# Half of the k and v loads moved to GpSimd's queue, in half batches, with a new order of work, in a linear-attention kernel with a gated convolution

## The chip, the cores and the metric

The kernel runs on one core of a Trainium2 chip. The metric is the device time of one execution in microseconds (us), here the median of three runs. A profile belongs to one execution; its "span" is the stretch between the first and the last instruction that the profiler saw.

The engines are called PE (matmul; PEld is its weight load), DVE (VectorE), ACT (ScalarE), POOL (GpSimd) and SP (SyncE, which issues transfers only). L12 is line 12 of the kernel's file.

## The reference

Two layers follow each other. Four batches, 8 heads, 768 steps, 48 channels a head:

```
for t in range(768):
    y[t]  = r[t] . (state + (u * k[t]) (x) v[t])      # per batch and head
    state = w * state + k[t] (x) v[t]                 # state is 48 x 48
x        = y, heads side by side: (4, 768, 384)
gate_pre = sum over 5 taps of conv_w[k] * x[t - 4 + k]    # causal
out      = (sigmoid(gate_pre) * (x @ w_val)) @ w_out      # both weights 384 x 384
```

Inputs and output are float32.

## The kernel before, in words

**Units.** A batch has three units of 256 steps, so there are twelve, n = 0 to 11; batch 0 is units 0 to 2, batch 1 is 3 to 5, batch 2 is 6 to 8 and batch 3 is 9 to 11. For units 2 to 11 a unit is two chunks of 128 steps; units 0 and 1 (n < TWO) place even and odd steps in neighbouring columns instead, which gives longer contiguous pieces in memory.

**What one unit needs**, by the names in the order string:

- `r:n`, `k:n`, `v:n`: loads of its rows into `r_st`, `k_st`, `v_st`. `k:4.1` is the second chunk of unit 4. A unit of r comes in pieces of 384 bytes (two steps); a chunk of k or v in 1,024 pieces of 192 bytes (one step of one head), L322.
- `RS`, `KS`: r and k times powers of the decay, to bf16 (L328, L342). `RT`, `KT`: transposes on PE (L353, L366); `RE`, `KE`: their copies out of PSUM (L297, L299).
- `PR`, `S`, `SE`: the bonus r.u.k (L402, L416). `DV`: v times this bonus (L430, L438). `CV`: v to bf16.
- `A`: attention scores within a chunk (L479), `M`: their mask (L489). `KV`, `ZI`, `ZE`: the running state (L516, L526, L536). `YD`, `YI`, `YZ`, `YE`: the unit's output from bonus, chunk and state (L561, L572), copied into `xT`.

**The second layer** works on seven pieces of up to 512 steps: `C` convolution (L664), `G` sigmoid (L675), `V` value product (L682), `HT` their product (L692), `O` output product (L705), `OE` its copy, `st` the store (L721); `OH`, `OF`, `sf` are the same in halves at the end (L732). `wv` and `wo` load the two weights, `WV` and `WO` cast them (`wval`, `wout`). `D:0.12` is filler on PE, twelve units of 128 columns (L737). `ER`, `EJ`, `EK` compute the tables of decay powers on ACT, from `w`. `CG` builds diagonal matrices for the convolution.

**What sets the order.** Every engine works in program order, and the whole program is one string, ORDER, found by a search and written out; each token is one stage. The ending names the engine: `/V` VectorE, `/P` GpSimd, `/A` ScalarE, `/S` SyncE; a number behind @ is the PSUM bank. An instruction that waits holds up everything behind it on its engine. A transfer's issue too is an instruction of its engine, so a load on SyncE's queue stands behind all earlier loads and stores there.

**Buffers.** `k_st` and `v_st` are rings of six tiles, a tile for one unit (NLD = 6, L61 to L65); `r_st` likewise. A load into a ring waits until the unit six before it has been read.

All loads and stores before are issued by SyncE, but for two stores at the end on ScalarE's queue.

Of the kernel before, what the change touches and what calls it, by code (L numbers as in the profile page):

```python
# [8 lines left out]
F32 = mybir.dt.float32  # L9
# [6 lines left out]
def kernel(  # L16
# [14 lines left out]
    B, H, S, D = r.shape  # L31
# [14 lines left out]

    TWO = 2
# [9 lines left out]
    def ring(name, shape, n, dtype=BF16):  # L57
# [245 lines left out]
    def pairs(t_):  # L303
        return t_.rearrange("p c h d -> p (c h d)").rearrange("p (h s d) -> p h s d", s=2, d=D)
# [33 lines left out]
    def scale_k(eng, n, c):  # L338
        if n < TWO:
            return scale_rows(eng, ks_t[n % NKS], pairs(k_st[n % NLD]), dj, c)  # L340
        cs = cut(c, 2)
        eng.tensor_tensor(  # L342
            out=ks_t[n % NKS][:, cs, :, :, 0:D].rearrange("p c n a d -> p c (n a) d"),
            in0=k_st[n % NLD][:, cs],
            in1=dk[:, cs],
            op=ALU.mult,
        )
# [80 lines left out]
    def bonus_v(eng, n):  # L428
        if n < TWO:
            return eng.tensor_tensor(  # L430
                out=dv_t[n % NDV].rearrange("p s (h d) -> p h s d", d=D),
                in0=pairs(v_st[n % NLD]),
                in1=s_t[n % NDV].rearrange("p s h -> p h s")[:, :, :, None].to_broadcast(
                    [128, H, 2, D]
                ),
                op=ALU.mult,
            )
        eng.tensor_tensor(  # L438
            out=dv_t[n % NDV].rearrange("p c (h d) -> p (c h) d", d=D),
            in0=v_st[n % NLD].rearrange("p c h d -> p (c h) d"),  # L440
            in1=s_t[n % NDV].rearrange("p s h -> p (s h)")[:, :, None].to_broadcast(
                [128, 2 * H, D]
            ),
# [290 lines left out]
    def dummy(m, b):  # L734
# [13 lines left out]
        w/S TE CD CP ML ZR/P ZV/V MK r:0.1/S k:0.0/S D:0.12@0 LN:.1 WS:.1@1 wp/S r:1/S r:0.0/S LN:.0 WS:.0@0  # L748
        SC ER:.2@1 k:0.1/S cw/S k:1/S u/S D:1.24@2 ER:.0@0 ZM/V ZK/V EJ:.3@1 ID r:2/S ER:.3@1 EK:.3@1
        RS:0.1/V k:2.0/S v:0/S k:2.1/S ER:.1@0 EJ:.2@1 EK:.2@1 v:1/S r:3/S k:3.0/S k:3.1/S EJ:.1@0 EJ:.0@0  # L750
        wv/S D:2.1@1 RS:1/V RT:0.1@3 EK:.1@0 v:2.1/S v:2.0/S k:4.1/S D:3.1@1 D:4.12@2 wo/S RS:0.0/V RT:0.0@1
        ZX/V RE:0.1@3/A r:4/S v:3.1/S k:4.0/S v:3.0/S RE:0.0@1/A KS:0.1/V KT:0.1@2 KE:0.1@2/A EK:.0@0 CB
        KS:0.0/V IT KT:0.0@3 KS:1/V k:5.0/S r:5/S v:4.0/S v:4.1/S WT@1 WC@1 RS:2/P KE:0.0@3/V CT@4 WM RT:1@5
        A:0.1@06 k:5.1/S CE@4 r:6/S PR:0.1@2 PR:0.0@3 k:6.0/S v:5.1/S k:6.1/S v:5.0/S UW@1 r:7/S k:7.1/S
        A:0.0@47 KT:1@2 RE:1@5/A S:0@1 CG:.0/P M:0.1@7 M:0.3@6 M:0.0@4 SE:0@1/A DV:0/P k:7.0/S RT:2@5 CV:0/A
        v:6.1/S v:6.0/S RE:2@5/A PR:1@2 D:5.2@1 D:6.12@7 M:0.2@0 KS:2/V KE:1@2/A S:1@7 CG:.2/P D:7.2@4
        YD:0@04 KV:0@51 ZE:0.0@5/V SE:1@7/V A:1.1@26 TS CV:1/A YI:0@04 M:1.2@2 KT:2@7 A:1.0@25 M:1.3@6
        YE:0.0@0/A ZI:0.1@1 RS:3/P YZ:0.1@4 KV:1@06 PR:2@7 DV:1/P KE:2@7/A S:2@3 ZE:0.1@1/V v:7.1/S k:8.1/S
        k:8.0/S r:8/S v:7.0/S ZI:1.0@0 M:1.1@5 RT:3@1 M:1.0@2 A:2.1@75 SE:2@3/A ZE:1.0@0/V M:2.3@5 CG:.1/P
# [24 lines left out]
        st:3.2/S ZE:7.1@6/V O:3.3@4 st:2.0/S O:3.1@0 M:8.1@1 CV:8/P KV:8.0@2 KS:9/P ZI:8.0@2 KT:9@6 KE:9@6/A
        OE:3.3@4/A st:3.3/S DV:8/P YD:8.0@1 M:8.2@5 ZE:8.0@2/V YD:8.1@3 OE:3.1@0/V YI:7.1@7 YI:8.0@1 PR:9@6
        YI:8.1@3 YZ:8.0@1 YZ:8.1@3 YZ:7.1@7 A:9.0@40 YE:8.0@1/A A:9.1@62 S:9@1 YE:8.1@3/A YE:7.1@7/V M:9.3@2
        M:9.2@6 O:3.0@3 RS:10/P RT:10@7 M:9.1@0 M:9.0@4 KS:10/P SE:9@1/V DV:9/P V:4.0@2 CV:9/A OE:3.0@3/A
        V:4.1@6 KT:10@0 RE:10@7/A KV:9.0@1 C:4@453 G:4.1@5 ZE:9.0@1/V KE:10@0/V PR:10@0 KV:9.1@1 V:4.2@7
        ZE:9.1@1/V S:10@5 YD:9.0@0 YD:9.1@1 YI:9.1@1 G:4.0@4 HT:4.1@6 st:3.0/S SE:10@5/A YI:9.0@0 YZ:9.1@1
        HT:4.0@2 G:4.2@3 YE:9.0@0/A HT:4.2@7 A:10.0@36 RS:11/P A:10.1@25 RT:11@0 M:10.0@3 CV:10/A O:4.3@7  # L790
        KV:10.0@3 ZI:10.0@3 M:10.2@2 RE:11@0/A ZE:10.0@3/V OE:4.3@7/A YE:9.1@1/A KS:11.0/P KT:11.0@4
        PR:11.0@4 DV:10/P KE:11.0@4/A O:4.1@2 OE:4.1@2/A O:4.2@0 M:10.1@6 KV:10.1@3 M:10.3@5 YD:10.1@1
        KS:11.1/P KT:11.1@7 YD:10.0@6 YZ:10.0@6 YI:10.0@6 YZ:10.1@1 YI:10.1@1 PR:11.1@7 KE:11.1@7/V S:11@5
        ZE:10.1@3/V YE:10.0@6/A YE:10.1@1/A A:11.0@67 M:11.1@7 SE:11@5/A DV:11/P st:2.3/S st:2.1/S st:4.3/S
        A:11.1@24 C:5@513 CV:11.0/A KV:11.0@7 OE:4.2@0/A V:5.2@0 M:11.0@6 ZI:11.0@7 G:5.1@1 V:5.1@1 G:5.2@3
        G:5.0@5 YD:11.0@3 V:5.0@5 M:11.3@4 YD:11.1@4 st:3.1/S YZ:11.0@3 M:11.2@2 HT:5.2@0 ZE:11.0@7/V
# [117 lines left out]
```

## Time and profile before

| | |
|---|---|
| median of three runs | 96.81 us (96.21 to 103.59) |
| the profiled execution | 96.63 us |
| its span | 94.9 us |
| read from HBM, written to it | 15.35 MB, 4.72 MB |
| loads of k in chunks, 192 KB each | 22 on SyncE's queue |
| loads of v in chunks, 192 KB each | 20 on SyncE's queue |
| stores, 192 KB each | 22 on SyncE's queue |
| busy on GpSimd: `rs` x10, `dv` x10 and x2, `ks` x7 and x2 | 18.2, 14.7 and 3.0, 12.7 and 2.0 us |

How to read the profile's lines. In the page's first part each engine has its busy time, its share of the span and its instructions. The second part cuts the span into 40 slices of 2.4 us; each digit is a busy share in tenths. A line of a group or a timeline names the line of code, the engine, the operation, the output and input tiles, shapes (partitions x elements) and a count; in brackets stands the idle time of the engine just before, and what ended it. "A <- B: 4.1, 3, 1.7" says that A waited for B for 4.1 us in total, three times, 1.7 us at most. An issue line ends with the median time from issue to landing. SPq is an issue on SyncE's queue.

### The profile page before, as it was taken

What the parts mean: (1) busy time and instruction counts of PE and PEld (TensorE: products, weight loads), DVE (VectorE), ACT (ScalarE), POOL (GpSimd) and SP (SyncE); (2) the same over time, 40 slices, a digit from 0 to 9 for tenths busy, and PEclk for the clock granted to TensorE, in tenths of its full rate; (3) what the DMA queues carried; (4) which work ended last, traced back from release to release, by engine and by line L of the source; (5) the groups of instructions that cost most, each with busy time, mean ns of one, the idle gap of its engine ahead of it and who ended that gap; (6) DMA issues with size and microseconds to landing.
All of it is one profiled execution on the core that took longest, in us unless ns stands there. A gap on an engine that the chain in (4) does not pass through costs nothing.

```text
span 94.9 us, 4608 instructions
## 1 busy us (share of the span) xinstructions
PE 84.0 (89%) x1973; PEld 58.9 (62%) x1979; DVE 78.6 (83%) x163; ACT 60.5 (64%) x119; POOL 59.7 (63%) x61
## 2 busy tenths in 40 slices
PE   5998977986795789799999899999999999999950
PEld 1545746755584456578757687587867778666630
DVE  5889999899455299989899969899997999989430
ACT  6597879784935646654797544835991897632740
POOL 6600499795809467698899899997918990800000
PEclk9999999999999999999999999999999999999999
DMA  0799999993759699898989999969997898950473
GB/s 4 191 297 310 284 267 226 214 276 67 199 149 270 128 261 211 200 219 170 258 175 215 231 259 211 228 179 271 224 240 161 286 228 316 364 200 11 166 286 129
DMA packets 62936, 20.36 MB, mean 214 GB/s; under 512 B 58814, under 2 KB 62916, under 8 KB 62916
## 3 DMA queue, kind: packets, MB, share of 16 engines
q1 hardware_dynamic: 62628, 19.88, 85.0%
q8 instruction: 15, 0.25, 1.1%
q10 hardware_dynamic: 288, 0.20, 0.6%
q14 instruction: 5, 0.04, 0.1%
HBM read 15.35 MB, written 4.72 MB: 211 GB/s over the span
## 4 chain that ended last, share of the span: by engine, by line
PE 37%; SPq 27%; DVE 12%; DMA 11%; POOL 4%; issue 4%; ACT 1%; ACTq 0%; POOLq 0%; DVEq 0%
SPq L322 16%; DMA k_st<-in_k_dram 11%; PE PS L705 7%; PE PS L572 6%; PE PS L682 6%; SPq L309 5%; PE PS L664 5%; POOL dv L438 3%; PE PS L479 3%; SPq L277 3%; DVE hT L692 3%; PE PS L561 2%; PE PS L353 2%; PE PS L516 2%; PE PS L366 2%
## 5 line engine op out<-in xcount | busy, mean ns | idle before, releaser
L489 DVE TENSOR_TENSOR at<-PS,mask 128x512 bf16<-128x512 f32 x48 | 30.4, 683 | 1.9 <-PE PS L479 1.4
L328 POOL TENSOR_TENSOR rs<-r_st,dr 128x768 bf16<-128x768 f32 x10 | 18.2, 1816 | 9.8 <-PE PS L353 6.8
L438 POOL TENSOR_TENSOR dv<-v_st,s_sb 128x768 bf16<-128x768 f32 x10 | 14.7, 1475 | 9.1 <-DMA v_st<-in_v_dram 4.1
L692 DVE TENSOR_TENSOR hT<-PS,gate 128x512 bf16<-128x512 f32 (+1 forms) x21 | 12.1, 610 | 4.4 <-PE PS L682 2.6
L705 PE MATMUL PS<-wout,hT 128*128 128x384 bf16 (+1 forms) x78 | 14.2, 314 | 1.5 <-POOL wout L299 1.0
L342 POOL TENSOR_TENSOR ks<-k_st,dk 128x768 bf16<-128x768 f32 (+1 forms) x9 | 14.7, 1635 | 0.9 <-DMA k_st<-in_k_dram 0.9
L297 ACT CAST xT<-PS 128x384 bf16<-128x384 f32 x20 | 9.0, 482 | 9.6 <-PE PS L572 9.4
L675 ACT ACTIVATE gate<-PS 128x512 bf16<-128x512 f32 (+1 forms) x21 | 10.3, 538 | 7.3 <-PE PS L664 6.6
L682 PE MATMUL PS<-xT,wval 128*128 128x512 bf16 (+1 forms) x57 | 13.8, 345 | 0.3
L297 ACT COPY rT<-PS 128x1024 bf16<-128x1024 bf16 (+1 forms) x13 | 12.3, 948 | 2.4 <-PE PS L353 2.4
L297 ACT COPY o<-PS 128x384 f32<-128x384 f32 (+1 forms) x19 | 8.5, 469 | 3.6 <-PE PS L705 3.5
L705 PEld LDWEIGHTS <-hT 128*128 128x128 bf16 x78 | 6.9, 97 | 5.4 <-issue 2.2
L297 ACT CAST vb<-v_st 128x768 bf16<-128x768 f32 (+1 forms) x10 | 8.0, 804 | 2.8 <-DMA v_st<-in_v_dram 2.6
L353 PE MATMUL PS<-ident,rs 128*128 128x128 bf16 x96 | 7.8, 224 | 0.9 <-POOL rs L328 0.9
L572 PE MATMUL PS<-at,vb 128*32 128x128 bf16 (+1 forms) x448 | 8.5, 220 | 0.0
L664 PE MATMUL PS<-xT,cwd 32*32 32x512 bf16 (+1 forms) x420 | 8.1, 346 | 0.0
L737 PE MATMUL PS<-some 128*128 128x512 bf16 (+2 forms) x19 | 6.8, 499 | 1.1 <-DVE some L142 1.1
L366 PE MATMUL PS<-ident,ks 128*128 128x128 bf16 x80 | 6.3, 219 | 1.4 <-ACT gate L675 0.9
L353 PEld LDWEIGHTS <-rs 128*128 128x128 bf16 x96 | 6.0, 100 | 2.5 <-POOL rs L328 1.1
L297 ACT COPY kT<-PS 128x1024 bf16<-128x1024 bf16 (+1 forms) x7 | 6.2, 890 | 1.9 <-PE PS L366 1.2
L682 PEld LDWEIGHTS <-wval 128*128 128x128 bf16 x63 | 5.4, 97 | 3.1 <-POOL wval L299 0.2
L536 DVE TENSOR_TENSOR z<-PS,bdm 128x384 bf16<-128x384 f32 x12 | 6.6, 553 | 1.0 <-PE PS L516 0.6
(89 smaller groups left out, 141.1 us busy)
## 6 DMA issues: line engine op xcount, KB each, us to landing
k_st<-in_k_dram SPq DMA_DIRECT2D x22, 192.0 KB, 4.3
r_st<-in_r_dram SPq DMA_DIRECT2D x11, 384.0 KB, 4.2
out_dram<-o SPq DMA_DIRECT2D x22, 192.0 KB, 3.8
v_st<-in_v_dram SPq DMA_DIRECT2D x20, 192.0 KB, 4.6
v_st<-in_v_dram SPq DMA_DIRECT2D x2, 384.0 KB, 5.1
wv_st<-in_moe_w_val_dram SPq DMA_DIRECT2D x1, 576.0 KB, 6.7
r_st<-in_r_dram SPq DMA_DIRECT2D x2, 192.0 KB, 3.5
k_st<-in_k_dram SPq DMA_DIRECT2D x1, 384.0 KB
```

Of the source, the lines that this page charges most:

```text
L297: eng.copy(out=dst, in_=src)
L322: q.dma_start(out=dst[n % len(dst)][:, c], in_=x[b, :, t0 : t0 + C, :].rearrange("h p d -> p h d"))
L328: eng.tensor_tensor(out=dst[:, :, ns, :, 0:D].rearrange("p s n a d -> p (n a) s d"), in0=src[:, hs], in1=tab[:, hs], op=ALU.mult,)
L342: eng.tensor_tensor(out=ks_t[n % NKS][:, cs, :, :, 0:D].rearrange("p c n a d -> p c (n a) d"), in0=k_st[n % NLD][:, cs], in1=dk[:, cs], op ...
L353: nc.tensor.transpose(bank16(b)[:, c0 : c0 + 128], src[:, s, i].rearrange("p a x -> p (a x)"), ident)
L438: eng.tensor_tensor(out=dv_t[n % NDV].rearrange("p c (h d) -> p (c h) d", d=D), in0=v_st[n % NLD].rearrange("p c h d -> p (c h) d"), in1=s ...
L489: nc.vector.tensor_tensor(out=at_t[n % NAT][:, c, a], in0=bank(b).rearrange("p (n x) -> p n x", x=128), in1=(mask2[:, c, None, :] if n < T ...
L572: nc.tensor.matmul(out=PS[32 * q : 32 * q + 32, b, 128 * T : 128 * T + 128], lhsT=lt, rhs=rh, start=False, stop=last, skip_group_check=True,)
L664: nc.tensor.matmul(out=halves(PS[32 * qo : 32 * qo + 32, b[T], 0:N], m), lhsT=cwd[rows, T, t, :], rhs=columns(xT[rows, T], m, PAD - t), st ...
L682: nc.tensor.matmul(out=halves(bank(b, N), m), lhsT=wval[:, kt, T, :], rhs=columns(xT[:, kt], m, 0), start=(kt == 0), stop=(kt == NT - 1),)
L692: nc.vector.tensor_tensor(out=hT_t[m % NHT][:, T, 0:N], in0=bank(b, N), in1=gate_t[m % NG][:, T, 0:N], op=ALU.mult,)
L705: nc.tensor.matmul(out=bank(b)[:, c], lhsT=hT_t[m % NHT][:, T, i * C : i * C + C], rhs=wout[:, T, c], start=(T == 0), stop=(T == NT - 1),)
```

## The change

The rings of k and v change from six tiles of a unit to two tiles of a batch (NLD = 2), with the head as the outer index within a partition. For units below BY = 6 a load writes its columns of the batch's tile, with the same pieces as before. For batches 2 and 3 a load brings four heads of a whole batch: `k:6.0`, `k:6.1`, `k:9.0`, `k:9.1` and the same of v, eight loads of 576 KB, each of 24 pieces of 192 bytes in each of the 128 partitions. They are issued by GpSimd, and so are six more loads: r:1, r:2, v:0, v:1, k:2.0 and k:3.1. The stages that read k and v take their columns from the batch's tile. The order string is a new one throughout; work has been handed between engines in it, too (`WO` and all of `WV` to ScalarE, `RS:3`, `RS:4`, `RS:10`, `DV:5`, `DV:8` to VectorE, the zeros of `rs` to VectorE and those of `xT` to GpSimd).

```
+    BY = 6
     TWO = 2
...
     NLD, NRL, NKS, NRS, NVB, NDV, NRT, NKT, NPR, NAT, NZ, NG, NHT, NO = (
-        6, 6, 3, 2, 4, 2, 3, 2, 2, 3, 6, 2, 2, 12
+        2, 6, 3, 2, 4, 2, 3, 2, 2, 3, 6, 2, 2, 12
     )
     r_st = ring("r_st", [128, H, 2, D], NRL, F32)
-    k_st = ring("k_st", [128, 2, H, D], NLD, F32)
-    v_st = ring("v_st", [128, 2, H, D], NLD, F32)
+    k_st = ring("k_st", [128, H, 2 * NU, D], NLD, F32)
+    v_st = ring("v_st", [128, H, 2 * NU, D], NLD, F32)
...
-    def pairs(t_):
-        return t_.rearrange("p c h d -> p (c h d)").rearrange("p (h s d) -> p h s d", s=2, d=D)
+    def unit(ts, n):
+        b, cu = divmod(n, NU)
+        return ts[b % len(ts)][:, :, 2 * cu : 2 * cu + 2, :]
+
+    def by_chunk(ts, n):
+        return unit(ts, n).rearrange("p h c d -> p c h d")
...
     def load_kv(dst, x, n, c, q):
         if n < TWO:
-            return load_rows(pairs(dst[n % len(dst)]), x, n, q, c)
+            return load_rows(unit(dst, n), x, n, q, c)
         b, cu = divmod(n, NU)
-        t0 = cu * W + c * C
+        if n < BY:
+            t0 = cu * W + c * C
+            return q.dma_start(
+                out=unit(dst, n)[:, :, c, :], in_=x[b, :, t0 : t0 + C, :].rearrange("h p d -> p h d")
+            )
+        hs = cut(c, H)
         q.dma_start(
-            out=dst[n % len(dst)][:, c], in_=x[b, :, t0 : t0 + C, :].rearrange("h p d -> p h d")
+            out=dst[b % NLD][:, hs].rearrange("p h c d -> p (h c) d"),
+            in_=x[b, hs].rearrange("h (c p) d -> p (h c) d", p=C),
         )
```

`scale_k`, `bonus_v` and `cast_v` read `unit(...)` or `by_chunk(...)` where they read `pairs(...)` or the tile itself.

GpSimd's queue in the new order, in program order (a colon marks a unit; loads in bold):

constants and masks, **r:1, v:0, r:2, k:3.1, v:1, k:2.0**, CV:0, RS:2, CG:.0, CG:.1, WM, DV:0, KS:2, CG:.2, **k:6.0**, KS:3, DV:1, DV:2, **v:6.1, v:6.0, k:6.1**, KS:5, DV:3, RS:5, DV:4, RS:6, KS:6, RS:7, CV:7, KS:7, **k:9.1, k:9.0**, KS:8, RS:8, DV:6, RS:9, DV:7, KS:9, **v:9.1, v:9.0**, KS:11.1, RS:11, KS:10, CV:11.1, KS:11.0, DV:9, DV:10, DV:11.

SyncE's queue begins with w, k:0.0, k:0.1, cw, k:1, wp, r:0.0, u, r:0.1, k:3.0, v:2.0, wv, k:4.0, k:2.1, wo, r:3, v:2.1, v:3.0, v:4.1, v:3.1, k:5.1, v:4.0, r:4, k:4.1, k:5.0, v:5.0, r:5, v:5.1, r:6; from there it holds r:7 to r:11 and the stores.

In the order before, the first real tokens and the last k and v loads were:

```
w/S TE CD CP ML ZR/P ZV/V MK r:0.1/S k:0.0/S D:0.12@0 LN:.1 WS:.1@1 wp/S r:1/S r:0.0/S LN:.0 WS:.0@0
...
M:6.0@4 O:2.2@4 ZI:5.0@1 M:6.2@3 RE:7@7/A O:2.1@3 KV:6.0@2 KS:7/P M:6.3@5 DV:5/P v:11.0/S M:6.1@6
OE:2.2@4/A OE:2.1@3/A v:11.1/S YD:5.0@5 YD:5.1@7 ZE:5.0@1/V KT:7@6 ZE:6.0@2/V PR:7@6 DV:6/P YD:6.0@1
```

More of the change, by code (lines that the diff above doesn't have):

```diff
@@ L339, in scale_k @@
         if n < TWO:
-            return scale_rows(eng, ks_t[n % NKS], pairs(k_st[n % NLD]), dj, c)
+            return scale_rows(eng, ks_t[n % NKS], unit(k_st, n), dj, c)
         cs = cut(c, 2)
@@ L343, in scale_k @@
             out=ks_t[n % NKS][:, cs, :, :, 0:D].rearrange("p c n a d -> p c (n a) d"),
-            in0=k_st[n % NLD][:, cs],
+            in0=by_chunk(k_st, n)[:, cs],
             in1=dk[:, cs],
@@ L431, in bonus_v @@
                 out=dv_t[n % NDV].rearrange("p s (h d) -> p h s d", d=D),
-                in0=pairs(v_st[n % NLD]),
+                in0=unit(v_st, n),
                 in1=s_t[n % NDV].rearrange("p s h -> p h s")[:, :, :, None].to_broadcast(
@@ L438, in bonus_v @@
         eng.tensor_tensor(
[L439 to L443, printed above, removed]
+            out=dv_t[n % NDV].rearrange("p c (h d) -> p c h d", d=D),
+            in0=by_chunk(v_st, n),
+            in1=s_t[n % NDV][:, :, :, None].to_broadcast([128, 2, H, D]),
             op=ALU.mult,
@@ L451, in cast_v @@
         if n < TWO:
-            return copy(eng, heads(vb_t[n % NVB]).rearrange("p s h x -> p h s x"), pairs(v_st[n % NLD]))
+            return copy(eng, heads(vb_t[n % NVB]).rearrange("p s h x -> p h s x"), unit(v_st, n))
         cs = cut(c, 2)
-        copy(eng, heads(vb_t[n % NVB])[:, cs], v_st[n % NLD][:, cs])
+        copy(eng, heads(vb_t[n % NVB])[:, cs], by_chunk(v_st, n)[:, cs])
     def attn2(n, s, b):
@@ L793 @@
[L793 to L796, printed above, removed]
-        CV:11.1/P YI:11.0@3 HT:5.0@5 HT:5.1@1 st:4.1/S st:4.2/S YZ:11.1@4 YE:11.0@3/V YI:11.1@4 O:4.0@5
@@ new lines @@
+        RT:2@5 M:0.3@7 ZE:0.0@4/V D:4.3@3 A:1.1@36 SE:0@2/A WV:.2/A A:1.0@27 M:0.0@0 CG:.1/P WM ZI:0.1@1
+        RE:2@5/A S:1@4 ZE:0.1@1/V WV:.0/A M:1.3@6 DV:0/P M:1.2@3 KS:2/P D:5.12@5 WV:.1/A CV:1/A WO:.2/A
+        YD:0@10 CG:.2/P YI:0@10 M:1.1@7 YZ:0.1@0 KV:1@36 M:1.0@2 RS:3/V YE:0.0@1/A YE:0.1@0/A KT:2@5
+        ZI:1.0@3 KE:2@5/A k:6.0/P ZE:1.0@3/V PR:2@5 C:0@201 SE:1@4/A V:0.2@7 D:6.4@4 ZI:1.1@6 k:4.1/S
+        G:0.2@1 G:0.1@0 ZE:1.1@6/V V:0.1@4 KS:3/P HT:0.2@7 V:0.0@0 A:2.1@51 A:2.0@63 S:2@7 k:5.0/S G:0.0@2
@@ L802 @@
+        sf:6.0/A
     """
```

96 lines of the change are left out of this document (47 added, 49 removed).

## The prediction

> **What bounds the kernel now.** I read the page's busy shares first, then its slices, then a table of five-microsecond stretches, then who waited in 20 to 50 us, then the DMA issues and the timelines of SyncE and GpSimd. The profiled execution took 96.63 us, for a span of 94.9 us and 1.7 us around it; the median of the three runs shown is 96.81 us, so the two stand within 0.2% and the sum below is made against 96.63.
>
> ```profile
> PE 84.0 (89%) x1973; PEld 58.9 (62%) x1979; DVE 78.6 (83%) x163; ACT 60.5 (64%) x119; POOL 59.7 (63%) x61
> POOL 6600499795809467698899899997918990800000
> DMA  0799999993759699898989999969997898950473
> q1 hardware_dynamic: 62628, 19.88, 85.0%
> ```
>
> Matmul is the fullest engine, and the DMA engines are nearly as full: one queue, q1, carries 62,628 packets. GpSimd has one hole, slices 3 and 4.
>
> ```profile
> 20.00:25.00 5.00, 3.80 (x129) 2.71 (x127) 3.84 (x7) 3.30 (x8) 3.63 (x4) 1.00 0.60 125
> 25.00:30.00 5.00, 3.86 (x153) 2.97 (x153) 3.35 (x7) 3.07 (x7) 2.58 (x6) 1.00 0.83 224
> 30.00:35.00 5.00, 3.87 (x80) 2.56 (x89) 2.62 (x5) 2.68 (x5) 3.27 (x3) 1.00 0.89 191
> 35.00:40.00 5.00, 4.49 (x103) 2.89 (x75) 5.00 (x10) 2.78 (x6) 2.98 (x3) 1.00 0.97 212
> 40.00:45.00 5.00, 4.94 (x131) 3.92 (x132) 4.53 (x9) 2.76 (x7) 4.69 (x4) 1.00 0.97 196
> ```
>
> The columns are the stretch, its length, busy us of PE, PEld, DVE, ACT, POOL, the granted clock, the DMA share and GB/s. PE lacks 1.20 + 1.14 + 1.13 + 0.51 = 4.0 us between 20 and 40 us. The same table has it lack 1.3 us in 10 to 20, 0.6 in 40 to 55, and next to nothing from 55 to 85. So what faster data can give lies before 55 us and is at most 5.9 us.
>
> ```profile
> POOL dv L438 <- DMA v_st<-in_v_dram: 4.1, 3, 1.7
> POOL wout L299 <- DMA wo_st<-in_moe_w_out_dram: 2.4, 1, 2.4
> DVE ks L342 <- DMA k_st<-in_k_dram: 2.4, 1, 2.4
> ACT vb L297 <- DMA v_st<-in_v_dram: 1.6, 1, 1.6
> POOL rs L328 <- DMA r_st<-in_r_dram: 1.0, 1, 1.0
> ```
>
> These are the longest waits for loads in 20 to 50 us: all stages that feed PE starve for data there. PE itself is then seen waiting for `wout` (1.0 us), `rs` (0.5), `ks` (0.5).
>
> ```profile
> k_st<-in_k_dram SPq DMA_DIRECT2D x22, 192.0 KB, 4.3
> 10.76 1.81 POOL L328 TENSOR_TENSOR rs<-r_st,dr 128x768 bf16<-128x768 f32 x1 [6.75 <-PE PS L353]
> 80.93 1.47 POOL L438 TENSOR_TENSOR dv<-v_st,s_sb 128x768 bf16<-128x768 f32 x1 [2.80 <-ACT s_sb L297]
> ```
>
> A chunk load lands a median 4.3 us after its issue. GpSimd stands idle for 6.75 us before its first real operation at 10.76, and its last `dv` ends at 82.4.
>
> **The change, part by part.** *Loads.* Thirty issues leave SyncE's queue and 14 appear on GpSimd's. Batches 2 and 3 were 24 chunk loads of 1,024 pieces of 192 bytes; they become eight loads of 3,072 such pieces. The six others (r:1, v:0, r:2, k:3.1, v:1, k:2.0) have 1,024 pieces each. Pieces and bytes stay the same, so the DMA engines' sum stays near 62.6 thousand packets; GpSimd's share is 6 x 1,024 + 8 x 3,072 = 30,720 of them.
>
> *What an issue costs GpSimd* is not in the trace. SyncE's issues of 1,024 such pieces of k last 0.38 us at the shortest, 1.0 at the median and 4.2 at the longest, the long ones being full of waiting for the engines. A GpSimd issue is therefore bounded by 0 (it runs beside the arithmetic) and 4.2 us for 1,024 pieces; for 3,072, by 0 and three times that, 12.7. I take the median for the small ones, 1.0, and 2.0 for a half batch, between three of the shortest (1.1) and three median ones (3.0), because one issue waits once and not three times. The Trainium skill's page "DMA: Bandwidth & Descriptors", section "Latency and other measured facts", gives about 1 us to the first byte on GpSimd's path; if that were an issue's whole cost, all 14 would be 14 us by estimate, below my 22.
>
> *Six small issues at the start.* They stand after the masks, where GpSimd's busy time ends at 4.0 (3.6 without the `rs` zeros, 0.56 us, which go to VectorE, and with two small memsets in their place). 6 x 1.0 ends at 9.6; CV:0 (0.82) ends at 10.4, and RS:2 follows, which began at 10.76. Covered by the 6.75 us hole: 0. If that cover is gone, each tenth above 1.1 us puts 0.6 us on RS:2, RT:2 and all behind; at 2.0 it is 5 us.
>
> *Work that leaves GpSimd.* RS 10 to 7 (3 x 1.816), DV 12 to 10 (2 x 1.476), the five `wval`/`wout` casts (2.1), `rs` zeros less the memsets that come (0.4); one KS more (1.816): 5.4 + 3.0 + 2.1 + 0.4 - 1.8 = 9.1 us less, 59.7 to 50.6. With issues 50.6 + 6 + 16 = 72.6, inside the 82.4 us it has. From 10.76 on, its arithmetic is 50.6 - 2.7 (head) - 0.8 (CV:0) = 47.1 us in 71.6; so 24.5 us are left for eight half batches, 3.1 each, if it never waits. Today it idles 71.6 - 56.0 = 15.6 us in that stretch, mostly for data; with half of that left, the point is at 2.1 each. My 2.0 lies just inside: 0.
>
> *Half batches in place.* k:6.0 follows CG:.2 and holds KS:3, DV:1 and DV:2 back by 2.0; v:6.1, v:6.0 and k:6.1 hold KS:5 by 6.0; k:9.1 and k:9.0 hold KS:8, v:9.1 and v:9.0 hold KS:11.1, by 4.0 each. Added up in program order from 10.4, KS:3 ends at 21.7 (22.7 today), DV:3 at 34.0 (35.0), KS:6 at 40.9 (46.0), KS:9 at 59.6 (63.6), DV:11 at 74.1 (82.4). The gap is what it has against waits. v:6.1 also waits until DV:2 and CV:2 have read batch 0's v, as the ring now holds two batches; behind it wait k:6.1 and KS:5, and behind them KT:5 on PE.
>
> *VectorE* takes three RS (0.96 each), two DV (near 1.0, the `ks` and `rs` rows) and gives up one KS (1.05) and, net, two whole and two half `kT` copies (2.2) and 0.8 of others: near +1 us of 78.6, with 16 us free: 0. *ScalarE* takes those `kT` copies (3.2) and the weight casts (2.1): near +6 on 60.5, free 34: 0 to 0.5 at a collision; I take 0.3. *PE* loses 14 of 68 units of filler (L737, 6.8 us for 68): nothing from the path, since they stood in idle time.
>
> *What comes earlier.* The v and `wout` casts that starved in 20 to 40 us are fed by two queues, and GpSimd's 24 chunk pieces stand no longer in SyncE's line. The bounds of the gain are 0 (same DMA engines, same pieces) and 5.9 (all PE idle gone). The nearest rows are the PE waits whose end is a stage named above as starved: 1.0 + 0.5 + 0.5 = 2.0, and I take 2.0. Against it 0.3 for ScalarE and 0.3 for the first half batch, whose 0.59 MB go ahead of r:3 and v:2.1 (2.8 us of transfer at 212 GB/s, mostly beside other work). Sum: 96.63 - 2.0 + 0.3 + 0.3 = 95.2 us.
>
> A rule speaks against even this. The Trainium skill, same page, section "Issuing engines are not separate DMA queues", says that all issuers end on the same 16 engines and a second one saves only issue time. The DMA share of 0.97 at 196 to 212 GB/s in 35 to 45 us agrees that the engines are full there; by the rule the sum would be 96.6 (2.0 of gain gone, the two 0.3 lost in the spread).
>
> **The rivals.** *A: GpSimd becomes the bound (slower).* The place is its queue from 17 us on; it decides from about 3 us for a half batch. For: 8 issues of 3,072 pieces on an engine that also does 50 us of arithmetic. Against: SyncE's uncrowded rate, 1.1. At 4 us the last `dv` ends at 10.8 + 47.1 + 32 = 90 in place of 82.4: 96.6 + 7.6 = 104 us; at 5.5, 116.
>
> *B: too much, too early (slower).* The four half batches of batch 2 (2.36 MB) go out between 17 and 33 us, before the rest of batch 1. The bytes to the end of batch 1 are then 1.2 weights + 7.1 + 2.4 = 10.7 MB; today 9.3 MB have passed by 45 us (the table's rates), so batch 1 is complete near 51, some 7 us after v:5.1 of today (issued at 40.7). Its v is not read before 46 (CV:5) and 51 (DV:5), and the new order runs KV:6 ahead of KV:5; so 3 to 4 us of the 7 show: near 100 us. Against: the order is laid round the early data.
>
> *C: nothing is gained*, the transfers being as slow as before and the work only moved: 96.6 us. For: the waits of the second table end at loads, and the pieces are the same. Against: 14 issues need not queue behind others any more. It is the case that the rule above describes.
>
> *D: two queues move more than one.* In 5 to 10 us the share reads 1.15 at 310 GB/s with pieces of 384 bytes, so engines can overlap packets. If all of PE's 5.9 us goes, with the two 0.3 as before: 91.3 us.
>
> **How the numbers follow.** Forecast 0.37, A 0.19, B 0.18, C 0.17, D 0.09. The forecast is 95.2 us, by itself 93.2 to 97.2. About 2% (1.9 us) is what a measurement here can tell from no change. Below 94.8 lie D and half of the forecast's lower side: 0.09 + 0.17 + 0.02 from B's favourable end = 0.28. Beyond 98.6 lie A and most of B: 0.19 + 0.15 + 0.01 = 0.35. The rest, 0.37, is within. The range runs from 92.0, into D, to 103.5, where A's upper half (about 0.10) is left out, with some 0.06 below.
>
> **What would show it.** Right: GpSimd's loads in the new profile as a queue of their own with about 30 thousand packets; RS:2 on GpSimd near 10.8; each half batch costing it 1 to 3 us; PE above 4.3 of 5 in the stretches 20 to 40; KS:6 near 41 to 46. Wrong: half batches over 3 us with PE waiting for GpSimd's `ks`, `rs`, `dv` (A); waits for `r_st` and `v_st` of batch 1 at 30 to 50 us on all engines (B); PE's shortfall before 40 us unchanged (C). If the small issues at the start cost over 1.1 us each, the whole order slides from RS:2 on, and the forecast is wrong whatever the half batches do.

## The result, and the profile after

The changed kernel took 113.62 us, the median of four executions (113.02 to 114.29), beside 97.62 us for the kernel before on the same chip. The ratio is 1.1775, with a 95% interval of 1.1621 to 1.1929: 16 us slower, where 95.2 us was forecast. The profiled execution took 114.29 us for a span of 112.3 us. (Some executions are disturbed and some per cent longer: the ratios leave them out, a median without a ratio stands where too few were left, and a time in square brackets is the median of the undisturbed ones alone.)

The page of the changed kernel: busy time of each engine, then the slices of GpSimd, of the granted clock of PE and of the DMA engines, then the two queues with packets, MB and share of the engines' time.

```profile
PE 90.3 (80%) x1967; PEld 62.2 (55%) x1974; DVE 85.8 (76%) x163; ACT 65.8 (59%) x128; POOL 68.3 (61%) x66
POOL 7994038799508992049999999999950081220000
PEclk9999999999995899995899999999999999999999
DMA  0999999599969999998629699819701602320074
q1 hardware_dynamic: 31428, 13.19, 45.8%
q0 software_dynamic: 1856, 6.69, 23.3%
```

Two things differ from the page before. GpSimd is busy for nine tenths or more of every slice from 19 to 29 (2.8 us each), and that run starts behind two holes, slices 12 and 17. And GpSimd's queue (q0) carries its 6.69 MB in 1,856 packets, 3.6 KB each, while SyncE's (q1) has 420 bytes a packet.

The table of stretches, with the columns as before (PE, PEld, DVE, ACT, POOL, granted clock, DMA share, GB/s):

```profile
10.00:15.00 5.00, 0.16 (x2) 0.00 (x0) 0.41 (x1) 0.58 (x1) 0.82 (x1) 1.00 1.12 271
15.00:20.00 5.00, 4.80 (x83) 4.08 (x84) 4.37 (x12) 3.32 (x6) 3.26 (x5) 1.00 1.13 260
20.00:25.00 5.00, 5.00 (x140) 3.10 (x138) 4.43 (x9) 4.07 (x11) 4.53 (x4) 1.00 0.73 192
25.00:30.00 5.00, 3.94 (x120) 2.75 (x110) 5.00 (x6) 3.36 (x8) 4.59 (x3) 1.00 1.09 234
30.00:35.00 5.00, 3.10 (x57) 2.24 (x51) 3.17 (x8) 2.45 (x5) 1.47 (x1) 0.88 0.81 161
35.00:40.00 5.00, 5.00 (x182) 3.90 (x177) 4.67 (x8) 3.49 (x7) 4.69 (x4) 0.78 1.04 233
...
45.00:50.00 5.00, 2.76 (x59) 1.84 (x58) 3.75 (x8) 2.28 (x4) 0.58 (x1) 1.00 1.06 229
50.00:55.00 5.00, 4.61 (x100) 3.45 (x96) 2.46 (x4) 1.81 (x3) 5.00 (x4) 0.66 0.88 247
...
75.00:80.00 5.00, 2.87 (x56) 1.51 (x29) 3.92 (x3) 2.88 (x5) 4.98 (x4) 1.00 0.90 212
```

In 10 to 15 us and in 45 to 50 us the DMA engines are full while PE and GpSimd starve. The packets of the trace, added up by queue, tell what is moved: 1.1 of the 1.4 MB in 10 to 15 us, and 1.4 of the 2.4 MB in 40 to 50 us, go through GpSimd's queue, while the loads that are waited for, r:0 and r:5, are SyncE's. The granted clock is lower around the holes at 30 to 35 us (0.88, then 0.78) and at 45 to 50 us (0.66 behind it), but behind the longest hole, at 10 to 15 us, it stays at 1.00.

PE's busy and idle time add up to the span. It is busy 6.3 us longer than before (90.3 against 84.0) and idle 11.1 us longer (22.0 against 10.9), 17.4 together, which is the difference of the spans. The mean granted clock fell from 1.000 to 0.969; by estimate that is worth up to 0.031 x 112.3 = 3.5 of the 6.3, and the rest of the 6.3 is not broken down here. Of the idle time, 4.5 us more lie in 5 to 20 us, 1.3 in 20 to 55, 4.9 in 55 to 85 and 0.3 at the ends.

The waits that matter, then GpSimd's timeline (the bracket is the idle time just before; the first line is the kernel before, the others are the changed kernel) and SyncE's issues of r:5 and r:6:

```profile
POOL dv L451 <- ACT s_sb L300: 10.5, 2, 6.6
POOL rs L341 <- DMA r_st<-in_r_dram: 6.6, 1, 6.6
PE PS L366 <- DVE rs L341: 5.0, 1, 5.0
```

```profile
36.05 1.82 POOL L328 TENSOR_TENSOR rs<-r_st,dr 128x768 bf16<-128x768 f32 x1 [1.02 <-DMA r_st<-in_r_dram]
```

```profile
15.96 1.81 POOL L341 TENSOR_TENSOR rs<-r_st,dr 128x768 bf16<-128x768 f32 x1 [4.56 <-PE PS L366]
...
24.11 1.46 POOL L334 DMA_DIRECT2D k_st<-in_k_dram  x1
...
35.30 2.87 POOL L334 DMA_DIRECT2D v_st<-in_v_dram  x2 [0.30 <-POOL dv L451]
38.16 1.42 POOL L334 DMA_DIRECT2D k_st<-in_k_dram  x1
...
49.42 1.80 POOL L341 TENSOR_TENSOR rs<-r_st,dr 128x768 bf16<-128x768 f32 x1 [6.56 <-DMA r_st<-in_r_dram]
...
90.20 2.91 POOL L451 TENSOR_TENSOR dv<-v_st,s_sb 128x768 bf16<-128x768 f32 x2 [6.56 <-ACT s_sb L300]
97.57 1.48 POOL L451 TENSOR_TENSOR dv<-v_st,s_sb 128x768 bf16<-128x768 f32 x1 [4.46 <-DVE s_sb L302]
```

```profile
36.28 0.73 SPq L316 DMA_DIRECT2D r_st<-in_r_dram  x1
...
38.13 7.51 SPq L316 DMA_DIRECT2D r_st<-in_r_dram  x1
```

SyncE issued r:5 at 36.28, just after GpSimd began to issue v:6.1, v:6.0 and k:6.1. It landed at 49.4, after 13.1 us; the kernel before issued it at 31.88 and began RS:5 at 36.05. SyncE's next issue but one, r:6, lasted 7.51 us, so its whole line stood. The PE wait of 5.0 us is the same thing at the start: the first products wait for the second half of r:0, issued by SyncE at 5.12, while GpSimd's six small loads pass it; it landed near 14.6, and RS:2 on GpSimd began at 15.96.

GpSimd's line shows nearly the whole loss. From 10.76 us, where RS:2 began before, to the end of its last `dv` it takes 88.3 us (to 99.05) in place of 71.6 (to 82.40), 16.7 more; the span is 17.4 longer. It is busy for 59.9 us of that in place of 56.1, though it now also issues the half batches (11.5 us), and idle for 28.4 in place of 15.6. The largest waits are those for r:5 (6.56 us), for `s_sb` (6.56, 4.46 and 3.92) and ahead of RS:2 (4.56).

### The profile page after: what moved, and what is told of

Same layout as the page of the kernel before. It is cut to its first block, busy times and chain, and to the rows that moved or that the text cites. A ratio compares the mean times of both kernels' runs of the same rounds, so it can differ in the third digit from the quotient of the medians.

```text
span 112.3 us, 4563 instructions
## 1 busy us (share of the span) xinstructions
PE 90.3 (80%) x1967; PEld 62.2 (55%) x1974; DVE 85.8 (76%) x163; ACT 65.8 (59%) x128; POOL 68.3 (61%) x66
## 3 DMA queue, kind: packets, MB, share of 16 engines
q0 software_dynamic: 1856, 6.69, 23.3%
## 5 line engine op out<-in xcount | busy, mean ns | idle before, releaser
L451 POOL TENSOR_TENSOR dv<-v_st,s_sb 128x768 bf16<-128x768 f32 x8 | 11.8, 1475 | 14.9 <-ACT s_sb L300 10.5
L341 POOL TENSOR_TENSOR rs<-r_st,dr 128x768 bf16<-128x768 f32 x7 | 12.7, 1812 | 11.1 <-DMA r_st<-in_r_dram 6.6
L355 POOL TENSOR_TENSOR ks<-k_st,dk 128x768 bf16<-128x768 f32 (+1 forms) x10 | 17.3, 1730 | 0.1
L716 PE MATMUL PS<-wout,hT 128*128 128x384 bf16 (+1 forms) x78 | 15.1, 322 | 0.1
L366 PE MATMUL PS<-ident,rs 128*128 128x128 bf16 x96 | 9.2, 249 | 5.7 <-DVE rs L341 5.0
L341 DVE TENSOR_TENSOR rs<-r_st,dr 128x768 bf16<-128x768 f32 (+1 forms) x6 | 8.3, 1397 | 5.7 <-DMA r_st<-in_r_dram 5.7
L366 PEld LDWEIGHTS <-rs 128*128 128x128 bf16 x96 | 7.0, 111 | 6.9 <-DVE rs L341 5.3
L300 ACT COPY kT<-PS 128x1024 bf16<-128x1024 bf16 (+1 forms) x11 | 9.4, 875 | 1.7 <-PE PS L379 1.6
L490 PE MATMUL PS<-rT,kT 48*128 48x128 bf16 x160 | 7.1, 218 | 3.8 <-issue 2.4
L415 DVE TENSOR_TENSOR pr<-PS,rT 128x1024 bf16<-128x1024 bf16 (+1 forms) x11 | 7.0, 635 | 3.0 <-ACT rT L300 1.6
```

The lines of the kernel that those rows point to most:

```text
L300: eng.copy(out=dst, in_=src)
L341: eng.tensor_tensor(out=dst[:, :, ns, :, 0:D].rearrange("p s n a d -> p (n a) s d"), in0=src[:, hs], in1=tab[:, hs], op=ALU.mult,)
L355: eng.tensor_tensor(out=ks_t[n % NKS][:, cs, :, :, 0:D].rearrange("p c n a d -> p c (n a) d"), in0=by_chunk(k_st, n)[:, cs], in1=dk[:, cs] ...
L366: nc.tensor.transpose(bank16(b)[:, c0 : c0 + 128], src[:, s, i].rearrange("p a x -> p (a x)"), ident)
L451: eng.tensor_tensor(out=dv_t[n % NDV].rearrange("p c (h d) -> p c h d", d=D), in0=by_chunk(v_st, n), in1=s_t[n % NDV][:, :, :, None].to_br ...
L716: nc.tensor.matmul(out=bank(b)[:, c], lhsT=hT_t[m % NHT][:, T, i * C : i * C + C], rhs=wout[:, T, c], start=(T == 0), stop=(T == NT - 1),)
```

## The experiments

Two theories stood after this reading. **Theory 1:** the second queue moves no more bytes; it changes whose bytes come first, and the half batches overtake what SyncE loads for batch 1. **Theory 2:** the half batches take GpSimd's time, 11.5 us, in a program order that has no room for it. Beside them stood a third suspect: products that VectorE took over and that collide with GpSimd's.

### The two queues by themselves

A kernel that computes nothing of the reference (it stores zeros): twelve chunk loads on SyncE alone, four half batches on GpSimd alone, chunks on GpSimd, both queues at once, then two-operand products and matmul streams.

```
+ for c in chunks: sync.dma_start(chunk of k)         # alone
+ for h in halves: gpsimd.dma_start(half batch of k)  # alone
+ both together; vector/gpsimd tensor_tensor alone and together; 200 matmuls alone, beside loads
```

> No part of the computation: zeros are stored, and stages are measured one after the other: 12 chunk loads by SyncE alone; four half batches by GpSimd alone (the same bytes); 12 chunk loads by GpSimd alone; SyncE's 12 and GpSimd's four together; a two-operand multiply on VectorE alone, on GpSimd alone, on both; 200 matmuls alone, beside SyncE's loads, beside GpSimd's. Theory 1: together, GpSimd's four land in little more than their time alone (near 10 us), and SyncE's chunks that were issued in the meantime land only after them. If the engines shared evenly, both streams would take near twice their time alone (near 20 us). Theory 3: VectorE's multiply takes 0.96 us alone and 2.5 to 2.8 beside GpSimd's; if it does not hold, 0.96 both times. Matmuls: if loads delay PE's instructions, gaps of 1 to 2 us stand in the stream beside GpSimd's loads and none in the stream alone.

The page's first line below is the rate in 40 slices of 3.7 us. SyncE alone (slices 5 and 6) gives 224 and 214 GB/s, GpSimd alone (slices 10 to 14, half batches and chunks) 216 to 219, and both together (slices 7, 8 and 15 to 17) 207 to 241. The timeline then shows the issues, and the small copies that wait for the loads ("mark"): alone SyncE needed 9.95 us for twelve issues, beside GpSimd's 17.86 us. The stages are not quite apart: GpSimd's first two half batches were issued at 21.05, beside SyncE's last chunks, and of the four that are to run beside SyncE's second twelve, two were issued at 47.47 already.

```profile
GB/s 0 0 0 49 224 214 241 207 9 217 217 219 216 217 209 227 208 194 222 58 2 0 0 0 0 0 0 0 4 0 159 207 170 275 281 306 301 392 393 52
```

```profile
12.93 9.95 SPq L50 DMA_DIRECT2D kt<-in_k_dram  x12
21.05 2.98 POOL L54 DMA_DIRECT2D kt<-in_k_dram  x2 [20.60 <-DVE mark L61]
...
47.47 2.82 POOL L54 DMA_DIRECT2D kt<-in_k_dram  x2 [0.57 <-DVE mark L61]
52.30 17.86 SPq L50 DMA_DIRECT2D vt<-in_v_dram  x12
52.48 2.83 POOL L54 DMA_DIRECT2D kt<-in_k_dram  x2 [2.20 <-DVE mark L61]
...
64.35 0.20 DVE L61 COPY mark<-kt 128x48 f32<-128x48 f32 x1 [6.91 <-DMA kt<-in_k_dram]
67.74 0.20 DVE L61 COPY mark<-vt 128x48 f32<-128x48 f32 x1 [3.20 <-DMA vt<-in_v_dram]
72.96 0.20 DVE L61 COPY mark<-vt 128x48 f32<-128x48 f32 x1 [5.02 <-DMA vt<-in_v_dram]
73.08 2.69 DVE L64 TENSOR_TENSOR da<-fa,fb 128x768 bf16<-128x768 f32 x3
76.14 5.31 POOL L64 TENSOR_TENSOR db<-fa,fb 128x768 bf16<-128x768 f32 x3
81.90 14.16 POOL L64 TENSOR_TENSOR db<-fa,fb 128x768 bf16<-128x768 f32 x6
81.98 14.90 DVE L64 TENSOR_TENSOR da<-fa,fb 128x768 bf16<-128x768 f32 x6 [0.32 <-POOL db L110]
```

So two queues move no more than one, and GpSimd's loads get the larger part: from 52.3 to 64.35 us, when its last half batch had landed, the packets of its queue carry 1.93 MB and those of SyncE's 0.72. SyncE's first six chunks had landed by 67.74 us and the last by 72.96. The products: 0.90 us each on VectorE alone, 1.77 on GpSimd alone, 2.48 and 2.36 when both run, nearly the sum of the two, as if one waited for the other. The 200 matmuls took 13.45 us alone, 11.34 beside SyncE's loads and 14.08 beside GpSimd's, the last with a granted clock of 0.50 to 0.62 at first; none of the three streams has gaps, so loads are not seen to hold up PE.

### Which part of the change costs, in the order of before

Five kernels keep the order of before and take one part of the change each.

```
e5   rings of two batch tiles, loads still by chunk (BY = 12), all on SyncE
g3   - r:1/S  v:0/S  r:2/S  k:3.1/S  v:1/S  k:2.0/S
     + r:1/P  v:0/P  r:2/P  k:3.1/P  v:1/P  k:2.0/P
h3   g3, and r:0.0/S directly behind r:0.1/S
g1   - k:6.0/S ... v:11.1/S (24 chunk loads)
     + KS:2/V k:6.0/P k:6.1/P ... KV:2.0@6 v:6.0/P v:6.1/P ... KS:5/P k:9.0/P k:9.1/P ... DV:5/P v:9.0/P v:9.1/P
g2   + RS:5/P k:6.0/P k:6.1/P v:6.0/P v:6.1/P ... RS:7/P k:9.0/P k:9.1/P ... DV:5/P v:9.0/P v:9.1/P
```

> The order and the queues of before, with only the new tiles: two tiles of a batch, head outermost, chunk loads throughout. If the layout itself costs (wider strides read by VectorE, GpSimd and ScalarE), the time rises by over 1 us; all theories expect 96.6 within 1 us.

> before with only the six small loads given to GpSimd, at the same places of the order, no half batch. Theory (bytes that overtake): their bytes are those that the first 20 us need anyway, but they overtake r:0 and k:1 on SyncE's queue, so the first r product comes 1 to 3 us later: 97 to 100 us. Rival (harmless, the loss is the halves and the order): 95.5 to 97. Rival (a freer SyncE queue helps, as the prediction counted): 94 to 95.5.

> before with the six small loads on GpSimd, and the second half of r of unit 0 issued directly behind the first one on SyncE. The 3.1 us that TensorE waits at 8.5 us should go: 92.5 to 95 us. Rival (given back later, as in the changed kernel): 96 to 97.5.

> The order of before, with its batch 2 and 3 loads of k and v replaced by the eight half batches on GpSimd, placed as soon as their tiles come free (k of batch 2 behind the third scaled k, v of batch 2 behind the third scaled v). Theory (the cost is the bytes that overtake): the two k halves, 1.15 MB, run at 20 to 30 us against batch 1's r, k and v; at about 250 GB/s they take 4.6 us from them, RS:5 starts near 39 to 42 instead of 36.05, and the time is 99 to 103 us. Rival (half batches on a second queue are harmless, the loss of the changed kernel is its other order): 95.5 to 97.5 us with RS:5 near 36. Rival (a half batch is dear by itself): 103 us or more, here and in the late form alike.

> The same, but the halves of batch 2 are issued only behind RS:5, those of batch 3 behind RS:7 and DV:5. Theory (bytes that overtake): nothing of batch 1 is overtaken, RS:5 stays near 36 us; the k halves are issued near 38 to 41 and land 8 us later, so KS:6, at 46 in before, comes 2 to 4 us late: 97 to 100 us, under the early form. Rival (a half batch is dear by itself): 103 us or more. Rival (harmless): 95.5 to 97.5.

The layout alone: 96.17 us, ratio 1.0069 (0.9968 to 1.0171). The six small loads alone: 96.50 us, 1.0062 (0.9983 to 1.0141); with r:0 ahead of them 96.34 us, 1.0011 (0.9953 to 1.0068), so the 1.0 us saved at PE's first wait (3.1 to 2.1 us) is not seen at the end (92.5 to 95 was expected of it). Neither part explains anything. The half batches alone: 114.44 us [110.88, one execution] placed early, and placed late 112.43 us [111.80], ratio 1.173 (1.152 to 1.194), beside 97.48 us [95.41]. The eight half batches by themselves cost 15 to 17 us, as much as the whole change; of the expectations, "dear by itself" came true in both forms.

The late form was to tell theory 1 from theory 2, and it spoke against theory 1 as the main cause in this order: RS:5 came on time (34.96 against 36.05), nothing of batch 1 was overtaken, and the time was lost all the same. GpSimd's timeline in the late form, and who waits for it:

```profile
34.96 1.81 POOL L341 TENSOR_TENSOR rs<-r_st,dr 128x768 bf16<-128x768 f32 x1 [1.31 <-DMA r_st<-in_r_dram]
36.72 3.01 POOL L334 DMA_DIRECT2D k_st<-in_k_dram  x2
39.72 2.83 POOL L334 DMA_DIRECT2D v_st<-in_v_dram  x2
42.56 1.49 POOL L451 TENSOR_TENSOR dv<-v_st,s_sb 128x768 bf16<-128x768 f32 x1
...
54.50 1.81 POOL L341 TENSOR_TENSOR rs<-r_st,dr 128x768 bf16<-128x768 f32 x1 [3.56 <-DMA r_st<-in_r_dram]
56.25 2.88 POOL L334 DMA_DIRECT2D k_st<-in_k_dram  x2
...
62.80 2.87 POOL L334 DMA_DIRECT2D v_st<-in_v_dram  x2 [0.41 <-POOL dv L451]
...
86.65 1.48 POOL L451 TENSOR_TENSOR dv<-v_st,s_sb 128x768 bf16<-128x768 f32 x1 [3.62 <-DVE s_sb L302]
```

```profile
PE PS L572 <- POOL dv L451: 11.6, 4, 4.6
```

GpSimd's last operation ends at 97.9 us against 82.85, 15.05 later, though RS:5 began 1.1 earlier. That is accounted for: the eight issues take 11.6 us, and idle time behind RS:5 grows by 4.6 (3.56 of it the wait for r:7, on SyncE's queue beside the half batches); 11.6 + 4.6 - 1.1 = 15.1. PE waits 11.6 us for `dv` behind them, against 0.7 before.

### GpSimd's time alone, and the same loads on other engines

```
h2   before, with eight memsets of an unread tile on GpSimd: RS:5/P (4), RS:7/P (2), DV:5/P (2)
h1   g1 with the eight half batches on SyncE (/S for /P)
h4   g2 with the eight half batches on ScalarE (/A for /P)
```

> before itself, with eight memsets of a tile that nothing reads, about 1.45 us each, on GpSimd at the places where the late form issues its half batches: no load is changed. If GpSimd's time is the cost: 104 to 109 us, since GpSimd has only some 8 us of idle time left from 36 us on and its last work stands 12 us before the end. If the loads are the cost: 97 to 99 us.

> The eight half batches in the order of before, at the places of the early form, but issued by SyncE; GpSimd issues nothing. If GpSimd's time for the issues is the cost: most of the 15 to 17 us goes, 97 to 102 us. If the form or the place of the load is the cost: 108 us or more, as with GpSimd.

> The late form of the half batches in the order of before, issued by ScalarE: still a second queue beside SyncE's, but no time of GpSimd. If GpSimd's time is the cost: 98 to 102 us. If a second queue that overtakes SyncE's loads is the cost: 107 us or more, with SyncE's r loads issued as late as in the GpSimd form (one issue of 9 us).

The idle work, with no load touched, took 111.94 us beside 96.59, ratio 1.1721 (1.1621 to 1.182). That is above the 104 to 109 expected, the memsets being longer than planned, 1.8 us each: they lasted 14.4 us (7.24 + 3.58 + 3.60) and cost 15.4. The last of the three fences below is from the kernel before:

```profile
39.31 7.24 POOL L807 MEMSET idle<- 128x2000 bf16 x4
...
55.78 3.58 POOL L807 MEMSET idle<- 128x2000 bf16 x2
...
62.51 3.60 POOL L807 MEMSET idle<- 128x2000 bf16 x2
...
87.38 1.48 POOL L439 TENSOR_TENSOR dv<-v_st,s_sb 128x768 bf16<-128x768 f32 x1 [3.63 <-DVE s_sb L300]
```

```profile
PE PS L562 <- POOL dv L439: 9.5, 4, 4.6
```

```profile
71.53 1.48 POOL L438 TENSOR_TENSOR dv<-v_st,s_sb 128x768 bf16<-128x768 f32 x1 [2.24 <-DVE s_sb L299]
```

GpSimd's time from 39 us on is on the path one for one in this order: RS:5 began 1.5 us late, before the first memset, and GpSimd's last operation ends 15.8 us late, so 14.3 us went with 14.4 us of memsets. VectorE was not slowed by them (79.3 us busy, 78.6 before). The kernel before shows 8.0 us of idle time on GpSimd after RS:5, and this one 8.5, so none of the extra work went into it. Of the 8.0, 5.0 are waits for `s_sb` (2.24 and 2.80): the first of them is 3.6 us in all these kernels and slides along with GpSimd's own lateness. The code gives the reason: `s_sb` comes from PE's bonus product of the `rs` and `ks` that GpSimd itself made. Such idle time is one engine waiting for its own results through others.

On SyncE the early form took 103.19 us [102.99], ratio 1.0757 (1.0536 to 1.0978), a little over the 97 to 102 expected, and 11.2 us less than the same loads at the same places on GpSimd (114.44; by the times in brackets 7.9 less). So most of the 11.6 us of issues shows up by a second way. The 6.6 us that stay are mostly a late load: k of batch 2 was issued at 40.35 and KS:6 had to wait for it, beginning at 49.72 (44.21 in before).

```profile
40.35 4.86 SPq L334 DMA_DIRECT2D k_st<-in_k_dram  x2
```

```profile
49.72 1.80 POOL L355 TENSOR_TENSOR ks<-k_st,dk 128x768 bf16<-128x768 f32 x1 [6.15 <-DMA k_st<-in_k_dram]
```

ScalarE as the issuer was a miss: 119.37 us, ratio 1.2473 (1.2296 to 1.265), expected 98 to 102. Two of its issues lasted 11.85 us and stood in front of its copies, and PE waited 14.3 us for one `xT`. It tells that ScalarE has no room for these issues at these places. Its time lies where the overtaking theory put it, but for this other reason, so it does not tell which theory holds.

### Parts undone in the changed kernel

```
e1   all 14 loads of GpSimd back on SyncE, same places
e2   the six small loads only        e3   the eight half batches only
f1   r:0.0/S r:0.1/S directly behind k:0.1/S
f2   v:6.1/P v:6.0/P k:6.1/P moved behind RS:5/P
g4   f1, and r:5/S directly behind r:4/S
e4   RS:3, RS:10, DV:8 back from /V to /P
i1   k:9.1 k:9.0 on SyncE behind r:8, v:9.1 v:9.0 on SyncE behind r:10
i2   g4 and i1 together
```

> The changed kernel with all 14 loads issued by SyncE in place of GpSimd, at the same places in the order; half batches stay. Theory 1 (GpSimd's loads are served ahead of SyncE's, and SyncE's land late for it): the idle 5 us at 10 to 15 us and the 6.6 us wait for r:5 are gone, and 113.6 us falls by 6 to 12, to 102 to 108. Theory 2 (it is the order and the early half batches, whatever queue carries them): within 3 us of 113.6. Theory 3 (VectorE and GpSimd block each other where both read two SBUF operands) says nothing on the queue: its three long VectorE operations (2.79, 3.54, 2.56 us) stay long under either.

> The changed kernel with only the six small loads given back to SyncE; the eight half batches stay on GpSimd. Theory 1: the wait for r:0 at 10 to 15 us goes (5 us), the wait for r:5 stays at 5 to 7 us; 113.6 falls to 107 to 110. Theory 2: SyncE then has more to issue at the start, RS and KS of units 1 and 2 come no earlier, and the time stays within 2 us of 113.6.

> The changed kernel with only the eight half batches given to SyncE; the six small loads stay on GpSimd. Theory 1: the wait at 10 to 15 us stays (5 us), the wait for r:5 (6.6 us) shrinks to under 3; 113.6 falls to 107 to 111. Theory 2: the half batches still stand ahead of r:5 in SyncE's own queue, r:5 lands near 49 us as before, and the time stays within 2 us of 113.6.

> The changed kernel, with SyncE issuing both halves of r:0 right after k:0, before GpSimd's first load goes out (it issued them at 3.95 and 5.12 us, GpSimd its first at 3.53). Theory 1 (GpSimd's loads overtake SyncE's that are issued beside or after them): r:0 lands by 8 us, the idle 5 us of PE at 10 to 15 us goes, and 113.6 falls by 4 to 6, to 108 to 110. Rival (the start has slack and another load is late next): under 2 us.

> The changed kernel, with the three half batches v:6.1, v:6.0 and k:6.1 issued by GpSimd after RS:5 in place of before KS:5. Theory 1: r:5 no longer stands behind 1.7 MB of them; GpSimd's wait for it falls from 6.6 us to under 2, RS:5 starts near 43 us in place of 49.4, and 113.6 falls by 2 to 5 unless KS:6 then waits for k:6.1. Rival: KS:6 and KV:6 wait for the half batches in its place, and the time stays within 2 us.

> The changed kernel, with RS:3, RS:10 and DV:8 on GpSimd in place of VectorE (1.81, 1.81 and 1.48 us more there). Theory 3 (the two block each other at two SBUF operands): the long VectorE operations of 2.79, 2.56 and 3.54 us are gone, PE's waits for DVE dv, z and hT (2.1, 1.1, 1.4 us) with them, and 113.6 falls by 2 to 5. Rival: GpSimd now holds its later work back by 1.8 us each time and the sum is within 2 us.

> The changed kernel with r of unit 0 directly behind the first half of k, and r of unit 5 directly behind r of unit 4 on SyncE's queue, ahead of the half batches of batch 2 in time. Theory (two late loads are the two large waits): both waits go, RS:5 starts near 40 to 43 instead of 49.4, and the time is 105 to 109 us. Rival (another load of batch 1 is late next, as when only r of unit 0 was moved): 111 to 114 us, with the wait now for k or v of unit 5.

> The changed kernel, with only the four half batches of batch 3 issued by SyncE (behind its loads of r of units 8 and 10), so that GpSimd is free of 5.75 us of issues between 60 and 76 us. If GpSimd is the path from 49 us on: 108 to 111 us. If it is not, or if the halves come too late on SyncE: 113 us or more, in the second case with a wait of the unit 9 products for k or v.

> The same on top of the changed kernel with r of units 0 and 5 early (110.66 us). If GpSimd is the path from 50 us on: 105 to 108 us. If not: 110 us or more.

Loads back on SyncE at the same places made it worse, where theory 1 expected 102 to 111: 120.39 us [116.76, one execution] (e1), 115.56 (e2, ratio 1.2147, 1.2071 to 1.2222) and 120.71 [118.00, one execution] (e3). The new order is laid for two queues: with one, v:0 stands far back in SyncE's line (PE waits 9.4 to 9.5 us for its cast in e1 and e2), or the casts of later v do (6.7 and 6.8 us in e1 and e3). These three say little on the cause.

f1 took the 5 us hole at the start away and gained nothing, 113.71 us [111.72, one execution, 1.175 times the 95.08 of before beside it]: RS:5 then waited 6.57 us for r:5 and began at 48.67 (49.42). g4 moved r:5 forward as well: RS:5 began at 44.10 with no wait, and the time was 110.66 us, ratio 1.1452 (1.125 to 1.1655), a gain of 3.0 where 5 to 9 was expected (3.1 by the ratios, whose intervals just overlap). f2 is not conclusive: its cast of v of unit 6 stands ahead of that load and takes what the tile held before, and the move put a 5.1 us wait for k of batch 2 into GpSimd's line; 121.14 us. e4 took the collisions away (`rs` and `dv` on VectorE had lasted 2.79, 3.54 and 2.56 us instead of 0.95, beside GpSimd's products) and gained nothing either: 113.83 us, ratio 1.1874 (1.1499 to 1.225). GpSimd then had those products to do (72.0 us busy against 68.3), which may have taken the gain back; that is not shown.

i1 freed GpSimd of 5.75 us of issues and gained 2.1 (3.7 by the ratios): 111.56 us [110.60], ratio 1.1388 (1.1136 to 1.164), just beyond the 108 to 111 expected, and in brackets inside it. On top of g4 it gained nothing: 110.93 us, 1.1416 (1.1194 to 1.1638). In i1 GpSimd, once free, waits for PE:

```profile
62.91 2.01 POOL L355 TENSOR_TENSOR ks<-k_st,dk 128x768 bf16<-128x768 f32 x1 [3.24 <-PE PS L527]
```

i1 shows one thing more. Up to 55 us its order is that of the changed kernel, and yet in its profile RS:5 began at 44.05 without a wait, and RS:6 behind it waited 2.78 us for its load. RS:6 began at 51.76 in i1, 51.88 in f1, 51.72 in e4 and 50.55 in g4, beside 52.61 in the changed kernel (42.08 in before): when one load comes in time, another load or PE holds the next product.

So in the changed kernel no single cause is the path from end to end.

## Why the prediction was wrong, point by point

**What an issue costs GpSimd: right, even too dear.** 1.0 and 2.0 us were taken; 0.88 to 1.06 and 1.42 to 1.46 were measured in the changed kernel.

**"My 2.0 lies just inside: 0" is the step that failed.** The working compared the sum of GpSimd's operations with the time that it has (24.5 us left, 15.6 of today's idle time, half of it usable) and let the half batches cost nothing. Its busy terms came out: 8.5 of the 9.1 us of arithmetic left GpSimd, and the issues took 11.5 and 5.6 us where 16 and 6 were set. What failed is the idle time in it: "with half of that left" leaves 7.8 us from 10.76 on, and 28.4 were measured; and of today's 15.6, put down mostly to data, 5.0 are waits for `s_sb`. So the line that was added up in program order ran late: KS:3 ended at 27.4 (21.7 worked out), DV:3 at 42.9 (34.0), KS:6 at 56.2 (40.9), KS:9 at 73.4 (59.6) and the last `dv` at 99.1 (74.1).

The idle time was no room. In the order of before, eight issues of 1.45 us cost 15 us, and idle work of 14.4 us cost 15.4. Rival A had the right place but the wrong condition, 3 us for a half batch: below that point it was to cost nothing, and in the order of before 1.45 us each was enough. How much the arithmetic handed to other engines was worth in the new order stays open.

**The first half batch, "0.3": mis-sized.** It was set against r:3 and v:2.1 by bytes shared at 212 GB/s. But SyncE's line stood while GpSimd's half batches passed: r:5 took 13.1 us in place of 4.2. Rival B named this (waits for `r_st` of batch 1 at 30 to 50 us) and priced it at 3 to 4 us; RS:5 came 13.4 us later than before. Undoing it together with the late r:0 (g4) gave 3.0 us, the size of B's price; B's 100 us is far off, since more than B was at work.

**The gain of faster data, 2.0: not there.** PE's idle time in 20 to 40 us fell from 4.0 to 3.0 us, and two of the four stretches stayed below the 4.3 of 5 that was named. Rival D is wrong: two queues together moved 207 to 241 GB/s, one alone 214 to 224. The Trainium skill's page "DMA: Bandwidth & Descriptors", section "Issuing engines are not separate DMA queues", states just this, and the runs agree with it. The same section calls the issuer's own time usually small beside the transfer; here 1.45 us stands beside 8 us to landing, as it says, and in the order of before it was still most of the loss, since the issuer was on the path.

**The six small loads, "covered by the 6.75 us hole: 0": right for the time, wrong for the place.** GpSimd had issued them by 9.1 us, but the loads passed r:0, PE stood 5.0 us, and RS:2 began at 15.96, not near 10.8. Alone in the order of before they cost nothing measurable.

**VectorE, "0": wrong in the trace, not seen in the time.** VectorE's busy time grew by 7.2 us (85.8 against 78.6) where +1 was worked out. Three products took 2.56 to 3.54 us in place of 0.95, beside products of GpSimd. The Trainium skill's page "SBUF — State Buffer", section "SBUF: two separate sides", tells of a port pair that the two hold by turns for a whole instruction; 0.90 and 1.77 us alone against 2.48 and 2.36 together agree. Giving the products back (e4) changed nothing.

**Packets: wrong.** GpSimd's queue was to carry about 30 thousand; it carried 1,856 of 3.6 KB.

What stays open: how the 16 us of the changed kernel divide. The half batches in the old order cost as much, 11.6 us of it as GpSimd's time in the late form; but in the new order the single repairs gave 0 (f1), 3.0 (g4), -0.2 (e4) and 2.1 us (i1), and two together no more than one. So that GpSimd's issues are the main part of the loss is shown for the old order only. No version was found that beats the kernel before; e5, g3 and h3 equal it.

## What to carry to other kernels

Idle time on an engine is room only if what it waits for doesn't depend on that engine; test it by putting idle work there before moving real work in. A second queue buys no bytes: it decides whose bytes come first, so list what stands in the other queue at that moment and when it is read. When an order found by search is changed in many places at once, try each part alone in the old order: that showed here which part is dear, while repairs within the new order were given back.

## What the hardware showed that was not expected

GpSimd's queue formed packets of 3.5 to 3.7 KB on average from pieces of 192 and 384 bytes, SyncE's 0.3 to 0.4 KB over all its transfers, and beside half batches on GpSimd SyncE's twelve issues took 17.86 us in place of 9.95 and its loads got 0.72 of 2.65 MB. That the large packets are why GpSimd's loads get more is argued from this, not shown. A load of 3,072 pieces cost GpSimd 1.42 to 1.59 us, one of 1,024 pieces 0.88 to 1.06. Issues on ScalarE beside a full SyncE queue lasted up to 11.85 us for two and held ScalarE's arithmetic. The granted clock of the changed kernel read 0.50 from 34 to 37 and from 51 to 54 us, behind holes of PE; the longer hole at 10 to 15 us was followed by 1.00, and these runs do not show what decides it.
